# A q load moved behind a transpose, and eight mask transfers moved to ScalarE's queue, in a decayed attention followed by a feed-forward layer

## The chip, the cores and the metric

The kernel runs on one core of a Trainium2 chip. The metric is the device time of one execution in microseconds. Before the change it is 207.12 us, the median of three runs (206.98 to 209.63).

## What is computed

A causal linear attention with a decay for each head is followed by a feed-forward layer with a parametric ReLU. Cut to what matters:

```
q, k, v: (4, 8, 768, 64)            # batch, heads, sequence, head size, float32
for each block of 64 positions:
    intra = ((q k^T) * lam^(i - j), zero above the diagonal) v
    inter = (q * lam^(i + 1)) state
    out   = intra + inter
    state = lam^64 * state + (k * lam^(63 - i))^T v
x = out as (3072, 512)
h = x @ w_in                        # (512, 2048)
g = max(h, 0) + alpha * min(h, 0)
result = g @ w_out                  # (2048, 512)
```

## The kernel before

The work is cut into 6 chunks of 512 rows of x. Chunk c holds 256 positions of two batches. A chunk's attention has four units, one for each batch of the chunk and each half of the heads: units 16 to 19 are chunk 4 (the last chunk but one), 16 and 17 its first batch, 18 and 19 its second.

For each unit, q and k are loaded as float32 (`load`, lines 82 to 102), cast to float16 (`cast`), transposed by a DMA (`transposes(n, "D")`, line 378), and q times its decay is formed from the transposed tile (`decayed`, L422). `cluster(old, new)` then runs on TensorE (PE): `inter(old)` (L442), the scores of the new unit (L472, or L460 in chunks 4 and 5), `intra(old)` (L506), and the new unit's state products (L526). VectorE (DVE) multiplies the scores with a mask (L487, L485) and updates the states R (L555); ScalarE (ACT) copies the old unit's result into xT (L298). `inter` of a unit reads states that the cluster before it has updated, so it also waits for that cluster's copy into xT and its updates of R.

The feed-forward layer fills the time between clusters: `up(c, f)` is four matmuls (L635) into one PSUM bank, ACT's negated ReLU `m` (L643) and DVE's combination `g` (L650), which frees the bank. The banks are "tk", "op" and two of "h". `down(c, t, part, 4)` is four matmuls with w_out (L663); after the last part ACT copies the sums out (L676) and SyncE's queue (SP) stores them (L679). The order on each engine is the order of the calls, which are written out by hand one after another up to chunk 2's end, and by a table `plan` after that. Each engine works through its list in order, and a DMA's issue is an instruction in the list of the engine that issues it.

Chunks 4 and 5 take the rows of a unit in another order than the others, and need masks in that order. `half_mask(0)` makes the first of them with four transfers from `dmask` into a tile of its own, which later units with the first half of the heads use; `half_mask(1)` makes the second with four transfers from `dmask` into the half of `dmask` that is no longer read after `masked(14)`. `later_half` (L264), on GpSimd (POOL), then fills the last quarter of each from the transferred part. Before the change all eight are issued by SP.

Transfers that SP and ACT issue report their end through eight semaphores that are handed out in turn to both queues together. A transfer is not issued before the previous one with the same semaphore has landed, so the issuing engine may wait for that at the place of the issue.

Names used below: T14 to T17 are the transposes of units 14 to 17; Q is the q load of chunk 4's second batch (512 KB) and K the four k loads of that batch (128 KB each); S1 and S2 are the stores after `down(1, 2, 3)` and `down(1, 3, 3)`; M0a to M0d are the four transfers of `half_mask(0)` and M1a to M1d those of `half_mask(1)`.

Of the kernel before, what the change touches and what calls it, by code (L numbers as in the profile page):

```python
# [11 lines left out]
def kernel(  # L12
# [16 lines left out]
    nc = tc.nc  # L29
    ctx.enter_context(tc.manual_schedule())  # L30
    fp32 = mybir.dt.float32
# [5 lines left out]
    B, H, S, D = q.shape  # L37
    assert (B, H, S, D) == (4, 8, 768, 64)
    L = 128
# [10 lines left out]
    raw_pool = ctx.enter_context(tc.tile_pool(name="raw", bufs=5))  # L50
# [31 lines left out]
    def load(c, bi, x, half=None, queue="S"):  # L82

        pb, b = c // 2, 2 * (c % 2) + bi
        if (c, bi) not in raws:
            raws[c, bi] = {}
        if x not in raws[c, bi]:
            raws[c, bi][x] = raw_pool.tile([128, H, 2 * D], fp32, tag=f"{x}raw", name=f"{x}raw")
        heads = ds(0, H) if half is None else ds(4 * half, 4)
        i = "kqv".index(x)  # L90
        if x == "k" and c >= HC:
            for a in range(2):
                for f in range(2):
                    nc.sync.dma_start(  # L94
                        out=raws[c, bi][x][ds(64 * a, 64), heads, ds(D * f, D)],
                        in_=k[b, heads, ds(pb * W + L * a + 64 * f, 64), :].rearrange("h p d -> p h d"),
                    )
            return
        (nc.gpsimd if queue == "G" else nc.sync).dma_start(  # L99
            out=raws[c, bi][x][:, heads, :],  # L100
            in_=(k, q, v)[i][b, heads, ds(pb * W, W), :].rearrange("h (p e) d -> p h (e d)", e=2),
        )
# [39 lines left out]
    def bank_of(bank, name, dtype=fp32):  # L142
        pool = h_ps_pool if bank == "h" else ps
        return pool.tile([128, CH], dtype, tag=bank, name=name)
# [25 lines left out]
    for half in range(2):  # L170
# [7 lines left out]
        out=drop, in0=rel_i, scalar1=0.0, scalar2=-1e30, op0=ALU.is_lt, op1=ALU.mult  # L178
# [65 lines left out]

    HM = {}

    def half_mask(hh):

        m = [dmask[:, x].rearrange("p l h a j -> p (l h) (a j)") for x in range(2)]
        if hh == 0:  # L250
            t = raw_pool.tile([128, H, 2 * D], fp32, tag="vraw", name="hmask")
            HM[0] = t.rearrange("p h d -> p (h d)")[:, 0:768].rearrange("p (x j) -> p x j", j=192)
        else:
            HM[1] = m[0]
        for a in range(2):
            for e in range(2):
                nc.sync.dma_start(
                    out=HM[hh][64 * a + e : 64 * a + 64 : 2, :, 0:L],
                    in_=m[hh][ds(64 * a, 32), :, ds(64 * (1 - e), L)],
                )  # L260

    def later_half(hh):

# [32 lines left out]
    def copy_on(eng, out, in_):  # L296
        if eng == "A":
            nc.scalar.activation(out, in_, AF.Copy)  # L298
        elif eng == "V":
            nc.vector.tensor_copy(out=out, in_=in_)  # L300
        else:
            nc.gpsimd.tensor_copy(out=out, in_=in_)  # L302
# [47 lines left out]
    def engine(x):  # L350
        return nc.gpsimd if x == "G" else nc.vector
# [21 lines left out]
    def transposes(n, eng, decay=True):  # L373

        t = T[n]
        qkT = qkt_pool.tile([128, 2, 2, 2, L], fp16, tag="qkT", name="qkT")
        if eng == "D":
            nc.sync.dma_start(  # L378
                out=qkT.rearrange("p x e h j -> p (x e h) j"),
                in_=t["qk16"].rearrange("p x e h d -> p (x e h d)"),  # L380
                transpose=True,
            )
        else:
            tp = ps.tile([128, 2, 2, 2, L], fp16, tag="tk", name="tp")
            for x in (1, 0):
                for e in range(2):
                    for hp in range(2):
                        nc.tensor.transpose(
                            tp[:, x, e, hp, :],
                            t["qk16"][:, x, e, ds(2 * hp, 2)].rearrange("p l d -> p (l d)"),  # L390
                            ident,
                        )
            copy_on(eng, qkT, tp)
            t["qps"] = tp[:, 0]
        t["qkT"] = qkT
        if decay:
            decayed(n)
# [19 lines left out]
    def decayed(n, eng="G"):  # L417
        c, bi, hh = units[n]
        t = T[n]
        qdT = qkt_pool.tile([128, 2, 2, L], fp16, tag="qdT", name="qdT")  # L420
        p = ds(64, 64) if c < 2 else ds(0, L)
        engine(eng).tensor_tensor(  # L422
            out=qdT[:, :, :, p],
            in0=(t["qps"] if eng == "P" else t["qkT"][:, 0])[:, :, :, p],
            in1=qdecay[:, hh, :, :, p],
            op=ALU.mult,
        )
        t["qdT"] = qdT
# [6 lines left out]
    def inter(n):  # L435
        co, bo, ho = units[n]
        pbo, bb = co // 2, 2 * (co % 2) + bo
        for a in range(2):
            if 2 * pbo + a == 0:
                continue  # L440
            for hp in range(2):
                nc.tensor.matmul(  # L442
                    ot[a][:, hp, :].rearrange("p (e j) -> p e j", e=2),
                    lhsT=R[bb, ho, 2 * pbo + a][:, hp].rearrange("p l d -> p (l d)"),
                    rhs=T[n]["qdT"][:, :, hp, ds(a * 64, 64)],
                    start=(hp == 0),
                    stop=False,
                    skip_group_check=True,
                )
# [118 lines left out]
    def cluster(old, new, eng="A"):  # L568

        if old is not None:  # L570
            inter(old)
        if new is not None:
            score_products(new)
        if old is not None:
            intra(old)
        if new is not None:
            state_products(new, kv_acc, old is None)
            masked(new)
        if old is not None:
            attended(old, eng)  # L580
        if new is not None:
            states(new, kv_acc)
# [47 lines left out]
    def up(c, f, bi=None, bank="h"):  # L630
        h_ps = bank_of(bank, "h_ps")
        n = CH if bi is None else W
        for gi in range(NHP):
            x = XT[c][:, gi]
            nc.tensor.matmul(  # L635
                h_ps[:, 0:n] if bi is None else h_ps[:, 0:n].rearrange("p (e j) -> p e j", e=2),
                lhsT=w_in_sb[:, gi, ts(f, 128)],
                rhs=x.rearrange("p e b j -> p (e b j)") if bi is None else x[:, :, bi, :],
                start=(gi == 0),
                stop=(gi == NHP - 1),  # L640
            )
        m = m_pool.tile([128, CH], fp32, tag="m", name="m")
        nc.scalar.activation(m[:, 0:n], h_ps[:, 0:n], AF.Relu, scale=-1.0)  # L643
        g = g_of(c, f)
        if bi is None:
            g, mv, hv = g.rearrange("p e b j -> p (e b j)"), m, h_ps
        else:
            g = g[:, :, bi, :]
            mv, hv = (y[:, 0:n].rearrange("p (e j) -> p e j", e=2) for y in (m, h_ps))
        nc.vector.scalar_tensor_tensor(  # L650
            out=g, in0=mv, scalar=oma[:, f : f + 1], in1=hv, op0=ALU.mult, op1=ALU.add
        )
# [4 lines left out]
    def down(c, t, part, nparts, bank="op"):  # L657
        if part == 0:
            O[c, t] = bank_of(bank, "o_ps")
        o_ps = O[c, t]  # L660
        n = NF // nparts
        for f in range(part * n, part * n + n):
            nc.tensor.matmul(  # L663
                o_ps,
                lhsT=lhs(c, f, t),
                rhs=w_out_sb[:, f, :],
                start=(f == 0),
                stop=(f == NF - 1),
            )
        if part == nparts - 1:  # L670
            store(c, t, o_ps, 0, DM)
            del O[c, t]
# [376 lines left out]
    cast(12, "q16", "G")  # L1049
    decayed(10, "G")  # L1050
    down(1, 1, 1, 4, "h")
    down(1, 0, 1, 4, "tk")
    load(4, 0, "q", 0)
    cast(13, "k16", "G")
    down(1, 2, 0, 4, "h")
    down(1, 2, 1, 4, "h")
    down(1, 1, 2, 4, "h")
    decayed(11, "G")
    cluster(9, 10, "A")
    cast(16, "q16", "G")  # L1060
# [20 lines left out]
    transposes(14, "D", False)  # L1081
    down(1, 2, 3, 4, "h")
    load(4, 0, "q", 1)
    half_mask(0)
    cast(15, "k16", "G")
    cast(17, "q16", "G")
    load_vh(4, 0, 0)
# [8 lines left out]
    key_decayed(17, "G")  # L1096
    up(2, 2, None, "h")
    up(2, 0, None, "tk")
    load(4, 1, "q", None)
    cast(17, "k16", "G")  # L1100
    decayed(14, "G")
    cast(16, "k16", "G")
    load_vh(4, 1, 0)
    cluster(12, 13, "A")
    load(4, 1, "k", None)
    transposes(16, "D", False)
    down(1, 3, 2, 4, "op")
    up(2, 1, None, "h")
    load_vh(4, 1, 1)
# [5 lines left out]
    key_decayed(18, "G")  # L1115
    cluster(13, 14, "A")
    down(1, 3, 3, 4, "op")
    half_mask(1)
    up(2, 10, None, "h")
    up(2, 13, None, "h")  # L1120
    up(2, 11, None, "op")
    cluster(14, 15, "A")
    up(2, 12, None, "h")
    up(2, 3, None, "tk")
    up(2, 6, None, "h")
    up(2, 9, None, "op")
# [111 lines left out]
```

## Time and profile before

| | |
|---|---|
| median of three runs | 207.12 us |
| the profiled execution's own time | 206.72 us |
| its span, first to last instruction | 204.9 us |
| PE busy | 198.6 us, 97% of the span |
| DVE busy | 154.9 us, 76% |
| POOL busy | 116.1 us, 57% |
| ACT busy | 113.8 us, 56% |
| clock granted to PE | full speed in all slices |

The views of the profile give times from the start of the span. Between span and execution time lie 1.8 us that no instruction of the kernel fills. A row of the timeline is: start, duration, engine, line, operation, names of output and inputs, count, and in brackets the idle time before it with what ended it. SPq and ACTq rows are issues of transfers; the transfer itself goes on after its issue.

### The profile page before, as it was taken

What the parts mean: (1) busy time and instruction counts of PE and PEld (TensorE: products, weight loads), DVE (VectorE), ACT (ScalarE), POOL (GpSimd) and SP (SyncE); (2) the same over time, 40 slices, a digit from 0 to 9 for tenths busy, and PEclk for the clock granted to TensorE, in tenths of its full rate; (3) what the DMA queues carried; (4) which work ended last, traced back from release to release, by engine and by line L of the source; (5) the groups of instructions that cost most, each with busy time, mean ns of one, the idle gap of its engine ahead of it and who ended that gap; (6) DMA issues with size and microseconds to landing.
All of it is one profiled execution on the core that took longest, in us unless ns stands there. A gap on an engine that the chain in (4) does not pass through costs nothing.

```text
span 204.9 us, 5641 instructions
## 1 busy us (share of the span) xinstructions
PE 198.6 (97%) x2271; PEld 121.2 (59%) x2271; DVE 154.9 (76%) x289; ACT 113.8 (56%) x212; POOL 116.1 (57%) x145
## 2 busy tenths in 40 slices
PE   7999999999999999999799999999999999999993
PEld 6776445556445465555454554467666666666883
DVE  6988889578789647899977679958888467675831
ACT  7986778144777118656486466654453544534320
POOL 8999893054478991299286957982085040553000
PEclk9999999999999999999999999999999999999999
DMA  5999999997999996899999995381001111011123
GB/s 165 278 196 234 248 264 207 234 293 230 230 261 282 201 231 156 226 154 218 180 242 140 263 151 79 65 128 37 18 0 54 51 54 51 3 51 55 62 88 110
DMA packets 67871, 31.71 MB, mean 155 GB/s; under 512 B 39860, under 2 KB 65604, under 8 KB 67844
## 3 DMA queue, kind: packets, MB, share of 16 engines
q1 hardware_dynamic: 48180, 21.64, 47.2%
q0 software_dynamic: 19360, 9.57, 33.0%
q8 instruction: 18, 0.29, 0.6%
q10 hardware_dynamic: 304, 0.13, 0.2%
q14 instruction: 9, 0.07, 0.1%
HBM read 27.27 MB, written 6.29 MB: 164 GB/s over the span
## 4 chain that ended last, share of the span: by engine, by line
PE 86%; DMA 4%; DVE 3%; SPq 3%; ACT 1%; issue 1%; ACTq 0%
PE h_ps L635 36%; PE o_ps L663 20%; PE o_ps L745 18%; DMA qkT<-qk 4%; PE acc L506 2%; PE s L472 2%; PE acc L442 2%; PE tpx L408 2%; SPq L94 1%; DVE dmask L212 1%; PE s L460 1%; PE acc L526 1%; SPq L378 1%; SPq L99 1%; ACT L190 1%
## 5 line engine op out<-in xcount | busy, mean ns | idle before, releaser
L650 DVE SCALAR_TENSOR_TENSOR g<-m,oma,h_ps 128x512 f16<-128x512 f32 (+1 forms) x98 | 71.4, 736 | 28.7 <-ACT m L643 25.5
L635 PE MATMUL h_ps<-xT,w_in_sb 128*128 128x512 f16 (+1 forms) x392 | 92.0, 375 | 0.0
L643 ACT ACTIVATE m<-h_ps 128x512 f32<-128x512 f32 (+1 forms) x98 | 57.3, 588 | 46.8 <-PE h_ps L635 35.9
L635 PEld LDWEIGHTS <-w_in_sb 128*128 128x128 f16 x392 | 37.6, 98 | 37.0
L663 PE MATMUL o_ps<-w_out_sb,g 128*128 128x512 f16 x192 | 46.8, 380 | 0.0
L745 PEld LDWEIGHTS <-g 128*128 128x128 f16 x296 | 28.2, 98 | 8.2
L663 PEld LDWEIGHTS <-g 128*128 128x128 f16 x192 | 17.6, 98 | 19.4 <-DVE g L650 0.2
L728 POOL TENSOR_TENSOR s<-g 128x512 f16<-128x512 f16 x11 | 12.8, 1168 | 28.4 <-PE o_ps L745 16.1
L487 DVE TENSOR_TENSOR sm<-s,dmask 128x1024 f16<-128x1024 f32 x16 | 19.6, 1222 | 11.7 <-PE s L472 11.7
L298 ACT ACTIVATE xT<-acc 128x512 f16<-128x512 f32 x24 | 14.3, 597 | 24.1 <-PE acc L526 22.1
L422 POOL TENSOR_TENSOR qdT<-qkT,qdecay 128x512 f16<-128x512 f16 (+1 forms) x19 | 20.1, 1065 | 7.9 <-DMA qkT<-qk 4.7
L745 PE MATMUL o_ps<-w_out_sb,g 128*128 128x256 f16 x192 | 24.1, 273 | 0.0
L302 POOL CAST qk<-qraw 128x512 f16<-128x512 f32 x12 | 8.5, 707 | 18.3 <-DMA qraw<-in_q_dram 17.8
L555 DVE SCALAR_TENSOR_TENSOR R<-R,rdecay,acc 128x128 f16<-128x128 f16 x54 | 15.5, 342 | 0.1
L728 POOL TENSOR_TENSOR g<-g 128x512 f16<-128x512 f16 x11 | 13.2, 1199 | 0.9
L777 ACT ACTIVATE o_sb<-o_ps 128x512 f32<-128x512 f32 (+1 forms) x15 | 7.5, 497 | 7.6 <-PE o_ps L745 7.6
L358 POOL TENSOR_TENSOR kdec<-kraw,kdecay 128x512 f16<-128x512 f32 x10 | 10.7, 1082 | 1.1 <-DMA kraw<-in_k_dram 1.0
L335 POOL DMA_DIRECT2D v<-in_v_dram x16 | 11.1, 701 | 0.4 <-issue 0.4
L745 PE MATMUL o_ps<-w_sum,g 128*128 128x256 f16 x88 | 11.3, 273 | 0.0
L780 DVE TENSOR_TENSOR o_sb<-o_sb,o_ps 128x512 f32<-128x512 f32 (+1 forms) x12 | 6.5, 550 | 4.2 <-PE o_ps L745 2.2
L302 POOL CAST qk<-kraw 128x512 f16<-128x512 f32 x9 | 5.5, 614 | 6.9 <-DMA kraw<-in_k_dram 6.9
L506 PE MATMUL acc<-sm,v 64*64 64x128 f16 (+1 forms) x384 | 9.2, 214 | 0.0
(95 smaller groups left out, 219.7 us busy)
## 6 DMA issues: line engine op xcount, KB each, us to landing
out_dram<-o_sb SPq DMA_DIRECT2D x20, 256.0 KB, 2.9
qraw<-in_q_dram SPq DMA_DIRECT2D x6, 512.0 KB, 6.2
w_in_sb<-in_moe_w_in_dram POOLq DMA_DIRECT2D x4, 512.0 KB, 7.9
w_out_sb<-in_moe_w_out_dram POOLq DMA_DIRECT2D x4, 512.0 KB, 10.5
kraw<-in_k_dram SPq DMA_DIRECT2D x16, 128.0 KB, 4.9
kraw<-in_k_dram SPq DMA_DIRECT2D x3, 512.0 KB, 4.2
qraw<-in_q_dram POOLq DMA_DIRECT2D x6, 256.0 KB, 7.1
qraw<-in_q_dram SPq DMA_DIRECT2D x6, 256.0 KB
```

Of the source, the lines that this page charges most:

```text
L298: nc.scalar.activation(out, in_, AF.Copy)
L302: nc.gpsimd.tensor_copy(out=out, in_=in_)
L422: engine(eng).tensor_tensor(out=qdT[:, :, :, p], in0=(t["qps"] if eng == "P" else t["qkT"][:, 0])[:, :, :, p], in1=qdecay[:, hh, :, :, p], ...
L487: nc.vector.tensor_tensor(out=t["sm"].rearrange("p a h x j -> p (a h) x j"), in0=t["s"].rearrange("p a h x j -> p (a h) x j"), in1=mask_of ...
L506: nc.tensor.matmul(o, lhsT=t["v16"][p, 2 * hp + hl, e, :], rhs=x, start=(2 * pb + a == 0 and hp == 0 and e == 0), stop=(e == 1), skip_grou ...
L555: nc.vector.scalar_tensor_tensor(out=R[b, hh, m + 1][:, hp], in0=R[b, hh, m][:, hp], scalar=rdecay[:, 2 * hh + hp : 2 * hh + hp + 1], in1= ...
L635: nc.tensor.matmul(h_ps[:, 0:n] if bi is None else h_ps[:, 0:n].rearrange("p (e j) -> p e j", e=2), lhsT=w_in_sb[:, gi, ts(f, 128)], rhs=x ...
L643: nc.scalar.activation(m[:, 0:n], h_ps[:, 0:n], AF.Relu, scale=-1.0)
L650: nc.vector.scalar_tensor_tensor(out=g, in0=mv, scalar=oma[:, f : f + 1], in1=hv, op0=ALU.mult, op1=ALU.add)
L663: nc.tensor.matmul(o_ps, lhsT=lhs(c, f, t), rhs=w_out_sb[:, f, :], start=(f == 0), stop=(f == NF - 1),)
L728: engine(eng).tensor_tensor(out=out, in0=in0, in1=in1, op=op)
L745: nc.tensor.matmul(t[:, cols], lhsT=x, rhs=w, start=(fresh and f == 0), stop=(last and f == NF // 2 - 1), skip_group_check=True,)
```

## The change

Two things are moved. Q stands behind T16 in SP's list instead of ahead of K and T16. The eight mask transfers are issued by ACT instead of SP: M0a to M0d after `down(1, 1, 1)` and the `down` calls behind it (before: all four by SP, after the second half of the q load of chunk 4's first batch), and M1a to M1d one by one after the `up` calls (2, 10), (2, 13), (2, 11) and (2, 12) (before: all four by SP, after S2). What the transfers move is the same.

```
-    def half_mask(hh):
+    def half_mask(hh, a, e):
...
-        for a in range(2):
-            for e in range(2):
-                nc.sync.dma_start(
-                    out=HM[hh][64 * a + e : 64 * a + 64 : 2, :, 0:L],
-                    in_=m[hh][ds(64 * a, 32), :, ds(64 * (1 - e), L)],
-                )
+        nc.scalar.dma_start(
+            out=HM[hh][64 * a + e : 64 * a + 64 : 2, :, 0:L],
+            in_=m[hh][ds(64 * a, 32), :, ds(64 * (1 - e), L)],
+        )
...
     down(1, 1, 1, 4, "h")
+    half_mask(0, 0, 0)
...
     down(1, 2, 0, 4, "h")
+    half_mask(0, 0, 1)
     down(1, 2, 1, 4, "h")
+    half_mask(0, 1, 0)
     down(1, 1, 2, 4, "h")
+    half_mask(0, 1, 1)
...
     load(4, 0, "q", 1)
-    half_mask(0)
...
-    load(4, 1, "q", None)
+    load(4, 1, "k", None)
...
-    load(4, 1, "k", None)
     transposes(16, "D", False)
+    load(4, 1, "q", None)
...
     down(1, 3, 3, 4, "op")
-    half_mask(1)
     up(2, 10, None, "h")
+    half_mask(1, 0, 0)
     up(2, 13, None, "h")
+    half_mask(1, 0, 1)
     up(2, 11, None, "op")
+    half_mask(1, 1, 0)
     cluster(14, 15, "A")
     up(2, 12, None, "h")
+    half_mask(1, 1, 1)
```

In the changed program the order of the list on ACT from 93 us of the profile before on is: m of up(2, 10), M1a, m of (2, 13), M1b, m of (2, 11), M1c, xT of unit 14, m of (2, 12), M1d, m of (2, 3), (2, 6) and (2, 9), xT of unit 15. The semaphores handed out in turn make M0d wait for the landing of the v load of chunk 3's first batch, M1a and M1b for the first and third of K, M1c for T16, and M1d for S2. SP's list there is: S1, T15, K, T16, Q, S2, T17.

More of the change, by code (lines that the diff above doesn't have):

```diff
@@ L245 @@
     HM = {}
-    def half_mask(hh):
+    def half_mask(hh, a, e):
         m = [dmask[:, x].rearrange("p l h a j -> p (l h) (a j)") for x in range(2)]
[L250 to L254, printed above, removed]
-        for a in range(2):
-            for e in range(2):
-                nc.sync.dma_start(
-                    out=HM[hh][64 * a + e : 64 * a + 64 : 2, :, 0:L],
-                    in_=m[hh][ds(64 * a, 32), :, ds(64 * (1 - e), L)],
-                )
+        if hh not in HM:
+            if hh == 0:
+                t = raw_pool.tile([128, H, 2 * D], fp32, tag="vraw", name="hmask")
+                HM[0] = t.rearrange("p h d -> p (h d)")[:, 0:768].rearrange("p (x j) -> p x j", j=192)
+            else:
+                HM[1] = m[0]
+        nc.scalar.dma_start(
+            out=HM[hh][64 * a + e : 64 * a + 64 : 2, :, 0:L],
+            in_=m[hh][ds(64 * a, 32), :, ds(64 * (1 - e), L)],
+        )
     def later_half(hh):
```

## Prediction

> **What bounds the kernel now.** I read the page's busy line first, then PE's waits, the chain that ended last, and then the timelines of the engines around the one wait that PE has.
>
> ```profile
> span 204.9 us, 5641 instructions
> PE 198.6 (97%) x2271; PEld 121.2 (59%) x2271; DVE 154.9 (76%) x289; ACT 113.8 (56%) x212; POOL 116.1 (57%) x145
> PE s L460 <- DMA qkT<-qk: 1.3, 1, 1.3
> 92.78 8.05 DMA qkT<-qk
> ```
>
> PE is idle for 204.9 - 198.6 = 6.3 us in all. The longest single wait is the 1.3 us for one transpose (third line, from PE's waits), whose transfer is on the chain for 8.05 us, from 92.78 to 100.83. The matmuls themselves are untouched by this change, so I expect nothing to be won beyond these 1.3 us. The question is whether they are won, and what the moved issues cost on their new engine.
>
> ```profile
> 95.75 3.63 PE L635 MATMUL h_ps<-xT,w_in_sb 128*128 128x512 f16 x16
> 99.22 0.39 PE L442 MATMUL acc<-qdT,R 128*128 128x128 f16 x4
> 100.87 0.37 PE L460 MATMUL s<-qkT 64*64 64x128 f16 x16 [1.27 <-DMA qkT<-qk]
> 101.52 1.90 PE L635 MATMUL h_ps<-xT,w_in_sb 128*128 128x512 f16 x8
> 105.85 0.39 PE L442 MATMUL acc<-qdT,R 128*128 128x128 f16 x4
> ```
>
> On PE the waiting instruction is the scores of unit 16, so the transpose is T16. The row at 95.75 is the four `up` calls (2, 12), (2, 3), (2, 6), (2, 9); 99.22 is `inter(15)`; the row at 101.52 begins with `up(2, 7)`, which uses bank "tk" after `up(2, 3)`. I take the start of `up(2, 7)`, 101.52, as the mark: by how much it moves, the end moves, as PE has no idle gap of note after it.
>
> **What holds T16.** The issues on SP, then POOL.
>
> ```profile
> 82.24 0.44 SPq L99 DMA_DIRECT2D qraw<-in_q_dram  x1
> 82.73 2.63 SPq L257 DMA_DIRECT2D hmask<-dmask  x4
> 85.47 0.54 SPq L679 DMA_DIRECT2D out_dram<-o_sb  x1
> 86.15 1.44 SPq L378 DMA_TRANSPOSE qkT<-qk  x1
> 87.63 1.42 SPq L99 DMA_DIRECT2D qraw<-in_q_dram  x1
> 89.09 3.51 SPq L94 DMA_DIRECT2D kraw<-in_k_dram  x4
> 92.78 2.80 SPq L378 DMA_TRANSPOSE qkT<-qk  x1
> 95.68 0.53 SPq L679 DMA_DIRECT2D out_dram<-o_sb  x1
> 96.31 3.58 SPq L257 DMA_DIRECT2D dmask<-dmask  x4
> ```
>
> ```profile
> 77.10 0.61 POOL L302 CAST qk<-kraw 128x512 f16<-128x512 f32 x1
> 85.59 0.61 POOL L302 CAST qk<-qraw 128x512 f16<-128x512 f32 x1 [7.88 <-DMA qraw<-in_q_dram]
> 92.03 0.62 POOL L302 CAST qk<-kraw 128x512 f16<-128x512 f32 x1
> 92.58 2.75 POOL L335 DMA_DIRECT2D v<-in_v_dram  x4
> 103.31 0.40 POOL L264 COPY dmask<-dmask 128x256 f32<-128x256 f32 x1 [4.46 <-DMA dmask<-dmask]
> ```
>
> SP works almost without a gap from 82 to 100 us, so its list decides when each issue comes. But T16 has a second condition: its k half is cast by POOL at 92.03 to 92.65, and T16 is issued at 92.78. Both are ready within 0.1 us of each other. POOL's list up to that cast starts when the q load issued at 82.24 lands (85.59), and that load is not moved.
>
> **The change part by part.** *SP loses M0 and, ahead of T16, Q.* That is 2.63 + 1.42 = 4.05 us: K is issued by about 88.6 instead of 92.6, as T15 has its cast since 77.7. T16 gains nothing at its issue, since the cast still ends at 92.65: I keep 92.65. What T16 gains is an emptier queue. Before, K and Q were issued in the 5 us ahead of it, and its issue alone took 2.80; now K has 4 us more to drain and Q comes behind.
>
> ```profile
> 67.12 1.24 SPq L378 DMA_TRANSPOSE qkT<-qk  x1
> 71.62 1.16 POOL L422 TENSOR_TENSOR qdT<-qkT,qdecay 128x512 f16<-128x512 f16 x1 [0.42 <-DMA qkT<-qk]
> DMA to landing us min/median/max: 3.8/5.9/6.4
> ```
>
> The quickest transpose with a known landing took 3.8 us from issue, the slowest 6.4 (the third row, all transposes of the trace for which it is known), T16 itself 8.05; the one issued at 67.12 let POOL go on at 71.62, 4.5 us later. Four v loads by POOL still run beside T16 (issued from 92.58). I take 4.5, so T16 lands at 97.2, with 96.45 and 100.7 as ends. By this PE's wait would be gone, as PE reaches the scores at 99.6.
>
> The Trainium skill, page "DMA: Bandwidth & Descriptors", section "Issuing engines are not separate DMA queues", speaks against this: transfers of all issuing engines run on the same 16 DMA engines and interleave, and another issuer saves issue time alone. By that rule alone T16 would take its 8.05 again, and the sum would be that of the second rival below. No row so far bears this out or against it: no two executions with another issuer can be compared yet.
>
> *M0 on ACT.* ACT is idle for 4.69 us where they stand:
>
> ```profile
> 62.65 1.52 SPq L99 DMA_DIRECT2D vraw<-in_v_dram  x2
> vraw<-in_v_dram SPq DMA_DIRECT2D x1, 512.0 KB, 5.5
> 68.24 0.60 ACT L643 ACTIVATE m<-h_ps 128x512 f32<-128x512 f32 x1 [1.56 <-PE h_ps L635]
> 73.52 0.60 ACT L298 ACTIVATE xT<-acc 128x512 f16<-128x512 f32 x1 [4.69 <-PE acc L526]
> ```
>
> M0d waits for a v load issued at 62.65 that takes 5.5, landing near 68.2, before ACT gets there at 68.84. Four issues at SP's price (2.63 / 4 = 0.66) end at 71.5; xT at 73.52 is not touched. ACT's own price of an issue is bounded below by nothing, where it lies beside the running activation, and above by the 2.80 that T16's issue took; 0.66, the same transfer on SP, is nearest. At the upper end four would need 11.2 us and delay xT, but no row shows a mask near that. Cost: 0. Their 256 KB run earlier, beside T11 and T12 instead of beside T15; POOL's idle 7.88 us before 85.59 takes up a delay of a microsecond there.
>
> *M1 on ACT.* This is where a wait is added. ACT's and DVE's rows:
>
> ```profile
> 93.22 0.60 ACT L643 ACTIVATE m<-h_ps 128x512 f32<-128x512 f32 x1 [0.27 <-PE h_ps L635]
> 94.94 0.60 ACT L643 ACTIVATE m<-h_ps 128x512 f32<-128x512 f32 x1 [0.27 <-PE h_ps L635]
> 95.88 0.60 ACT L298 ACTIVATE xT<-acc 128x512 f16<-128x512 f32 x1 [0.34 <-PE acc L526]
> 97.37 1.11 DVE L555 SCALAR_TENSOR_TENSOR R<-R,rdecay,acc 128x128 f16<-128x128 f16 x4
> 103.22 0.75 DVE L650 SCALAR_TENSOR_TENSOR g<-m,oma,h_ps 128x512 f16<-128x512 f32 x1 [0.36 <-ACT m L643]
> ```
>
> M1a and M1b (behind 93.22 and the next m) wait for parts of K that were issued 4 us or more earlier: they cost 0.66 each, partly inside the 0.27 gaps, and ACT reaches M1c at about 96.3 instead of 95.5. M1c waits for T16. Until 97.2 ACT stands, with xT of unit 14, and behind it DVE's updates of R (they come after that copy), and so `inter(15)`, queued. From T16's landing on: issue 0.66, xT 0.60, R 1.11, `inter(15)` 0.39, the rest of the cluster 101.52 - 100.87 = 0.65, and three hand-overs of 0.05 (T16's landing at 100.83 let PE start at 100.87): 3.56 in all. So `up(2, 7)` could start at 97.2 + 3.56 = 100.8, 0.7 earlier than before. This alone would still be a gain.
>
> M1d waits for S2. S2 is now issued behind T16 (1.3) and Q (1.42): about 95.4, the same as before. Behind M1d on ACT stand m of `up(2, 3)`, whose g frees bank "tk" for `up(2, 7)`. From S2's landing: issue 0.66, m 0.60, g 0.75, hand-overs 0.15: 2.16.
>
> ```profile
> DMA to landing us min/median/max: 2.3/2.3/2.3
> DMA to landing us min/median/max: 6.0/6.0/6.0
> 92.00:102.00 10.00, 8.73 (x129) 4.72 (x128) 9.60 (x18) 5.75 (x11) 6.85 (x10) 1.00 1.62 201
> ```
>
> When does S2 land? The first row is the store issued at 79.77, with little beside it: 2.3. The second is S2 itself in the trace: 6.0. So 97.7 and 101.4 are the ends. Between them I go by the bytes: from 92.65 on T16 (256 KB), four v loads (64 KB each), Q (512 KB), S2 (256 KB) and M1a and M1b (128 KB), together 1.44 MB in bytes, have to pass, and the third row shows 201 GB/s in these 10 us: 7.2 us, hence 99.85. A lone store of 262 kB needs 1.3 at that rate and took 2.3, so 1.0 of a transfer is not rate; half of that, as the queue runs already, gives 100.3, also the nearer to S2's own row. Then `up(2, 7)` starts at 100.3 + 2.16 = 102.46, later than the 100.8 of the other chain: +0.94 us.
>
> *What is late next.* xT of unit 15 follows m of (2, 3), (2, 6), (2, 9) and ends near 103.3, when `up(2, 7)` ends. M1d lands 3.8 after its issue (the median of the second masks; worst 5.4):
>
> ```profile
> DMA to landing us min/median/max: 3.0/3.8/5.4
> 103.67 2.28 POOL L422 TENSOR_TENSOR qdT<-qkT,qdecay 128x512 f16<-128x512 f16 x2
> ```
>
> From 100.3 that is 104.1; POOL's copy (0.40) and the first qdT (1.14) end at 105.7, before `inter(16)` at 105.85 + 0.94. T17 is issued earlier, near 96, and K is already in: no loss there.
>
> **Sum.** -1.26 (PE's wait on T16, 101.52 - 100.26, the time at which PE is ready when nothing holds it: 99.22 + 0.39 + 0.65), +2.20 (the wait moved to `up(2, 7)` through ACT, 102.46 - 100.26): +0.94 us on a span of 204.9, so 205.8; with the 1.8 around it 207.6 for that execution. The runs' median stands 0.4 above the profiled execution, so I forecast 208.0.
>
> **Rivals.** *First, the gain arrives.* If S2 lands by 98.0, both chains end before PE is ready at 100.26, with T16 at its quick end of 96.45: 1.26 saved, 205.9. S2 at 98.7 saves 0.7, at 99.36 nothing. For it: K is out of the way 4 us earlier, and a store alone took 2.3. Against it: Q now stands between T16 and S2, and POOL's loads do not move. Centre 206.5.
>
> *Second, slower.* T16 stays as slow as it was, 8.05, because the DMA engines and not the order of issue set its time. It lands at 100.7, ACT stands there, and Q and S2 (0.79 MB at 201 GB/s, 3.9 us) follow: S2 at 104.6, `up(2, 7)` at 106.8, +5.2 us: 212.3. It decides from T16's landing at 98.0 on, where 98.0 + 3.56 passes 101.52 whatever S2 does; with S2 at its old 6.0 it is +2.0, 209.1. Against it: T16's time held K's and Q's remainder, which is gone.
>
> *Third, the masks come too late.* M1d issued at 100.3 takes the worst 5.4: POOL's qdT ends at 107.3, `inter(16)` 0.5 later still: +1.4, 208.5.
>
> **How the numbers follow.** Forecast 0.50 (207.2 to 209.1), gain 0.30 (205.9 to 207.1), second rival 0.12 (209.1 to 212.3), third 0.08. The range is 206.0 to 210.0: it holds the forecast, the third rival, nearly all of the gain and the near end of the second. A difference of 2%, 4.1 us, is about what a measurement of this kernel can tell from no change. A gain of that size is three times PE's whole wait: 0.01. A loss of that size needs the far half of the second rival: 0.05. Within 2%: 0.94.
>
> **What would show it.** Right: PE's wait for the transposed tile at the scores of unit 16 is gone or under 0.3; T16 is issued near 92.7, in about 1.3, and lands near 97; ACT is idle before M1c until T16's landing and before M1d until S2's; PE waits before `up(2, 7)` for g. T16 issued before 92 would show that POOL's cast did not hold it. Wrong: ACT not idle at M1c and M1d, a T16 of 8 us, or an end moved by more than `up(2, 7)` moved, which would mean a cost that I have not seen.

## The result and the profile after

The changed kernel takes 214.29 us (median of four runs, 213.6 to 214.65), the kernel before 207.05 us on the same chip. The ratio is 1.036, 95% interval 1.032 to 1.040: slower by 3.6%. The forecast was 208.0, with a range of 206.0 to 210.0; the direction was right and the size was not. The profiled execution took 214.65 us, with a span of 212.9: 8.0 more than before. Medians are of all executions, and ratios leave out those over 1.5% above the fastest of their kernel.

The page of the kernel after, its busy line and its slices, and PE's waits:

```profile
span 212.9 us, 5638 instructions
PE 202.0 (95%) x2271; PEld 123.1 (58%) x2271; DVE 156.8 (74%) x289; ACT 113.7 (53%) x212; POOL 115.7 (54%) x145
PEclk9999999999999999999669999999999999999999
PE h_ps L634 <- DVE g L649: 3.3, 1, 3.3
PE acc L441 <- DVE R L554: 1.2, 1, 1.2
```

PE's wait for the transposed tile (1.3 us) is gone from its list. In its place stand two waits, 1.2 and 3.3 us. And there is something that was in no slice of before: PE's clock falls to 0.6 in two slices. PE is busy 3.4 us longer with the same 2271 matmuls, as some of them ran slower: in the warm-up, and where the clock fell.

The timeline of PE in the kernel after, around the mark of the prediction, `up(2, 7)`:

```profile
96.44 3.63 PE L634 MATMUL h_ps<-xT,w_in_sb 128*128 128x512 f16 x16
101.26 0.38 PE L441 MATMUL acc<-qdT,R 128*128 128x128 f16 x4 [1.19 <-DVE R L554]
101.99 0.29 PE L525 MATMUL acc<-v,kdec 64*64 64x64 f16 x8
105.62 3.57 PE L634 MATMUL h_ps<-xT,w_in_sb 128*128 128x512 f16 x8 [3.34 <-DVE g L649]
108.99 1.49 PE L662 MATMUL o_ps<-w_out_sb,g 128*128 128x512 f16 x4
110.31 1.03 PE L634 MATMUL h_ps<-xT,w_in_sb 128*128 128x512 f16 x4
```

Against the rows of before this gives the ledger. The `up` calls at 95.75 begin at 96.44: 0.7 of the difference had arisen by 10 us in the warm-up and belongs to the execution (other executions below have between 0.0 and 0.6 there). `inter(15)` waits 1.19 for R. `up(2, 7)` begins at 105.62 instead of 101.52: +4.1. Its eight matmuls take 3.57 instead of 1.90 us, and the row of 104.12 comes at 110.31: +6.2. So 2.1 us are the clock; all four executions of this kernel have a mean granted clock of 0.982 to 0.984. Up to PE's last matmul another 0.3 is added. The last 1.5 lie behind it, in the final stores (4.8 us from PE's end at 208.1 to the span's end, 3.3 before), and no other execution profiled here has them. Without the start's 0.7 and these 1.5 the ledger comes to 5.8 us, while the four executions lie 6.5 to 7.6 above the 207.05 of the kernel before; what the other three lose beyond the 5.8 is not shown.

The clock fell early in the longer stretch:

```profile
103.00:104.00 1.00, 0.00 (x0) 0.00 (x0) 0.00 (x0) 0.00 (x0) 0.00 (x0) 0.54 1.32 182
```

The third figure from the end is the clock. It was full up to 103 and averages 0.54 from 103 to 104, so it had halved about 0.8 us after PE stopped at 102.28. The stretch of 1.19 us just before it may count too.

ACT's timeline of the kernel after shows where the waits come from, and the chain that ended last names their first link:

```profile
94.84 0.61 ACTq L256 DMA_DIRECT2D dmask<-dmask  x1
98.64 0.61 ACTq L256 DMA_DIRECT2D dmask<-dmask  x1
99.36 0.60 ACT L297 ACTIVATE xT<-acc 128x512 f16<-128x512 f32 x1 [3.07 <-PE h_ps L634]
103.48 0.61 ACTq L256 DMA_DIRECT2D dmask<-dmask  x1
104.19 1.57 ACT L642 ACTIVATE m<-h_ps 128x512 f32<-128x512 f32 x3 [3.75 <-DMA out_dram<-o_sb]
```

```profile
95.66 7.79 DMA out_dram<-o_sb
103.48 0.61 ACTq L256
104.19 0.60 ACT m L642
104.82 0.76 DVE g L649
105.62 3.57 PE h_ps L634 x8
```

M1c is issued at 98.64 and M1d at 103.48. Ahead of M1c ACT stands 3.07 us; PE, which the row names, had been done long before, so the releaser is another: T16, whose semaphore the issue waits for and which landed at 98.62 by the events in the trace. Ahead of M1d it stands 3.75 us, and there the row names the store. S2 was issued at 95.66 and was under way for 7.79 us.

### The profile page after: what moved, and what is told of

It is laid out like the page before. It is cut to its first block, busy times and chain, and to the rows that moved or that the text cites. A ratio compares the mean times of both kernels' runs of the same rounds, so it can differ in the third digit from the quotient of the medians.

```text
span 212.9 us, 5638 instructions
## 1 busy us (share of the span) xinstructions
PE 202.0 (95%) x2271; PEld 123.1 (58%) x2271; DVE 156.8 (74%) x289; ACT 113.7 (53%) x212; POOL 115.7 (54%) x145
## 4 chain that ended last, share of the span: by engine, by line
PE 89%; DMA 4%; DVE 2%; ACT 2%; ACTq 1%; issue 0%
PE h_ps L634 38%; PE o_ps L662 19%; PE o_ps L744 17%; DMA out_dram<-o_sb 4%; PE unread L162 3%; PE acc L505 2%; PE s L471 2%; PE acc L441 2%; PE tpx L407 2%; DVE w_sum L710 1%; DVE g L649 1%; PE acc L525 1%; PE s L459 1%; ACT L190 1%; ACT m L642 1%; PE p L744 0%
## 5 line engine op out<-in xcount | busy, mean ns | idle before, releaser
L634 PE MATMUL h_ps<-xT,w_in_sb 128*128 128x512 f16 (+1 forms) x392 | 93.6, 380 | 3.5 <-DVE g L649 3.3
L421 POOL TENSOR_TENSOR qdT<-qkT,qdecay 128x512 f16<-128x512 f16 (+1 forms) x19 | 21.2, 1119 | 6.6 <-DMA qkT<-qk 3.2
L301 POOL CAST qk<-qraw 128x512 f16<-128x512 f32 x12 | 7.6, 630 | 16.2 <-DMA qraw<-in_q_dram 15.4
L441 PE MATMUL acc<-qdT,R 128*128 128x128 f16 x80 | 8.4, 219 | 1.4 <-DVE R L554 1.2
```

The costliest lines, as they stand in the source:

```text
L421: engine(eng).tensor_tensor(out=qdT[:, :, :, p], in0=(t["qps"] if eng == "P" else t["qkT"][:, 0])[:, :, :, p], in1=qdecay[:, hh, :, :, p], ...
L441: nc.tensor.matmul(ot[a][:, hp, :].rearrange("p (e j) -> p e j", e=2), lhsT=R[bb, ho, 2 * pbo + a][:, hp].rearrange("p l d -> p (l d)"), r ...
L634: nc.tensor.matmul(h_ps[:, 0:n] if bi is None else h_ps[:, 0:n].rearrange("p (e j) -> p e j", e=2), lhsT=w_in_sb[:, gi, ts(f, 128)], rhs=x ...
```

## The experiments

**What belongs to which part.** Four kernels on one chip, beside a kernel before of 206.79 us. The first moves Q alone:

```
 load(4, 1, "k", None)          # kernel before; was: load(4, 1, "q", None)
 ...
 transposes(16, "D", False)
+load(4, 1, "q", None)
```

> The kernel before, with Q alone moved behind T16; all masks stay on SP's queue. Theory (the loss is ACT standing at M1c and M1d): ACT issues nothing here, so nobody waits for S2. T16 is still held by POOL's cast until about 92.7 but has K and no Q ahead of it, so PE's wait of 1.27 us for it shrinks: 205.8 to 207.0 us. Rival (Q in front of S2 is bad by itself, whoever waits): 209 us or more.

Measured: 207.14 us, ratio 1.005 (1.001 to 1.008). PE and the chain of this kernel:

```profile
99.61 0.37 PE L460 MATMUL s<-qkT 64*64 64x128 f16 x16
105.69 0.38 PE L442 MATMUL acc<-qdT,R 128*128 128x128 f16 x4 [0.93 <-POOL qdT L422]
```

```profile
98.49 5.26 DMA dmask<-dmask
104.30 1.35 POOL qdT L422
```

```profile
DMA to landing us min/median/max: 7.8/7.8/7.8
```

The wait for T16 is gone; the scores begin at 99.61 instead of 100.87. But the masks behind Q and S2 land at 103.75 (98.49 + 5.26), POOL's qdT is late, and `inter(16)` gives 0.93 back. The last row is S2 here: 7.8 us, as in the kernel after, but no computing engine waits for it. So Q's place makes S2 late, and by itself it gives back through the masks about what it wins. By the median the rival (209 and more) falls, and the theory was 0.1 us too low. Three of the ten executions took 208.67 to 209.54, which this trace, of the fastest, does not explain.

The second kernel is the changed one with Q back in its old place:

```
-load(4, 1, "k", None)
+load(4, 1, "q", None)
 ...
+load(4, 1, "k", None)
 transposes(16, "D", False)
-load(4, 1, "q", None)
```

> The kernel after, with Q back ahead of K and T16; the masks are issued by ACT as in the changed kernel. By the turn of the semaphores M1c now waits for the last part of K, long landed, and M1d still for S2, which has no Q ahead of it any more. Theory (the loss is S2's late landing seen through M1d, and T16's seen through M1c): S2 is issued near 94 to 95 and lands within 3 to 6 us, so up(2,7) starts between 100 and 103 instead of 105.6, PE's idle stays under 2.5 us and the clock full: 206.5 to 208.5 us. Rival (eight transfers on ACT's queue cost it by themselves): 212 us or more.

Measured: 210.17 us, ratio 1.017 (1.013 to 1.021): between the two. ACT, PE and DVE of this kernel:

```profile
100.54 0.61 ACTq L256 DMA_DIRECT2D dmask<-dmask  x1
```

```profile
102.68 1.89 PE L634 MATMUL h_ps<-xT,w_in_sb 128*128 128x512 f16 x8 [2.04 <-DVE g L649]
107.68 0.38 PE L441 MATMUL acc<-qdT,R 128*128 128x128 f16 x4 [0.52 <-POOL qdT L421]
```

```profile
112.69 4.54 DVE L710 TENSOR_TENSOR w_sum<-w_out_sb 128x512 f16<-128x512 f16 x1
```

M1d goes out at 100.54, three microseconds earlier than in the kernel after, and `up(2, 7)` starts at 102.68 with a gap of 2.04 and at full clock, all as the theory had it. The number missed by 1.7, through two delays further on. The masks cost 0.5. And a w_sum on DVE takes 4.54 us; g stands behind it, and PE waits 1.3 us for that. In the kernel before DVE has for the same operation:

```profile
110.86 0.42 DVE L711 TENSOR_TENSOR w_sum<-w_out_sb 128x512 f16<-128x512 f16 x1
```

By the medians Q alone costs 0.35 us and the masks alone 3.4; together they cost 7.2. So about 3.5 us come only when both are moved: Q directly ahead of S2, and M1d behind S2.

The third kernel leaves M0 on ACT and Q behind T16, and gives M1 back to SP:

```
 down(1, 3, 3, 4, "op")
+half_mask(1, ...) x4 on nc.sync
 ...                            # the four calls on nc.scalar taken out
```

> The kernel after, with the second masks M1a to M1d back on SP behind S2; M0 stays on ACT and Q behind T16. Theory: neither ACT nor PE waits for T16 or S2 at M1; PE's old wait of 1.27 us for T16 is gone too: 205.6 to 206.4 us, PEclk full between 100 and 110 us. Rival (Q's place or M0 on ACT carries part of the loss): 208 us or more.

Measured: 209.59 us median of 12 runs (206.61 to 210.09), ratio 1.006 (1.003 to 1.010); the profiled execution took 209.91. The median lies in the rival's range. PE's row and a window behind it:

```profile
107.36 0.38 PE L441 MATMUL acc<-qdT,R 128*128 128x128 f16 x4 [2.29 <-POOL qdT L421]
```

```profile
108.00:110.00 2.00, 2.00 (x36) 0.86 (x22) 1.47 (x3) 0.60 (x1) 2.00 (x3) 0.56 1.38 219
```

Both waits of ACT are gone, as the theory had it, and `up(2, 7)` starts at 100.58. Then the masks, again last behind Q and S2, hold qdT of unit 16, PE waits 2.29 us, and the clock falls to 0.56. So Q's place carries part of the loss, as the rival had it, through the masks. Late masks are what the prediction's third rival was about, with a chance of 0.08, though by a slow M1d on ACT.

The trace stands for the slower executions alone: seven of the twelve took 209.55 to 210.09 at a mean clock of 0.989 to 0.992, and five took 206.61 to 208.20 at 0.998 to 1.0. In this trace T16 was issued at 93.86, against 92.73 with Q alone moved, and all that follows on SP came later too; whether M0 on ACT has a share in that was not tried.

The fourth keeps M1 on ACT, but so early that by the turn of the semaphores it follows transfers that have landed. (There M1 overwrites a mask that unit 14's scores still use, so part of the computation is changed.)

```
 later_half(0)
+half_mask(1, 0, 0); half_mask(1, 0, 1); half_mask(1, 1, 0); half_mask(1, 1, 1)
```

> The kernel after, with M1a to M1d written behind the first half's copy, ahead of up(2,10); they stay on ACT. Their places in the turn of the semaphores now follow S1, T15 and the first two parts of K, all landed by then. Theory (the wait, not the queue, is the cost): four issues of 0.6 us beside the activations, no ACT idle over 1 us in 90 to 104, PE's wait for T16 gone: 205.6 to 206.8 us. Rival (masks on ACT's queue in this stage cost PE by themselves): 209 us or more.

Measured: 209.4 us, ratio 1.011 (1.007 to 1.015). The number is the rival's; the trace shows that the kernel is no test of it. ACT, then PE, then DVE of this kernel:

```profile
91.12 2.63 ACTq L256 DMA_DIRECT2D dmask<-dmask  x4
93.86 0.60 ACT L297 ACTIVATE xT<-acc 128x512 f16<-128x512 f32 x1 [2.20 <-DMA dmask<-dmask]
```

```profile
95.00 1.02 PE L634 MATMUL h_ps<-xT,w_in_sb 128*128 128x512 f16 x4 [0.36 <-ACT o_sb L675]
98.33 0.40 PE L441 MATMUL acc<-qdT,R 128*128 128x128 f16 x4 [2.31 <-DVE R L554]
99.35 5.31 PE L634 MATMUL h_ps<-xT,w_in_sb 128*128 128x512 f16 x16
```

```profile
96.02 1.23 DVE L486 TENSOR_TENSOR sm<-s,dmask 128x1024 f16<-128x1024 f32 x1 [3.58 <-PE h_ps L634]
97.16 1.11 DVE L554 SCALAR_TENSOR_TENSOR R<-R,rdecay,acc 128x128 f16<-128x128 f16 x4
```

No issue waits. The four of them in a row keep ACT for 2.63 us, xT starts at 93.86, and PE waits 0.36 us at 95.00 for what ACT does next. PE's 2.31 us have another cause. DVE's masking of unit 14 now stands behind the four transfers that write its mask, and waits for all of them: by the events in the trace the last landed at 95.94, and the masking starts at 96.02. The matmul that its row names is not what it needs. R follows at 97.16 and `inter(14)` at 98.33, and the 16 matmuls behind it run at a lower clock: 5.31 us instead of 3.63. So the 2.31 us are not the price of issues on ACT, and this kernel leaves open what issues without a wait cost PE beyond the 0.36 us.

**Which wait.** One slot earlier in the order, M1d follows T16 instead of S2; the four transfers and ACT's queue are the same.

```
 down(1, 3, 3, 4, "op")
+half_mask(1, 0, 0); half_mask(1, 0, 1)
 up(2, 10, None, "h")
+half_mask(1, 1, 0)
 up(2, 13, None, "h")
+half_mask(1, 1, 1)
```

> The kernel after, with the second masks on ACT a little earlier in the order: M1a and M1b right behind down(1,3,3), M1c behind up(2,10), M1d behind up(2,13). By the turn of the semaphores M1a now follows S1, M1b and M1c parts of K, all landed, and M1d follows T16 instead of S2. Theory (it is the semaphore's turn that chains ACT to S2): ACT stands once, until T16 lands near 98, not until S2 near 103; inter(15) starts near 102, PE's idle is one gap of about 2 us and no second one before up(2,7): 207.5 to 210.5 us, the upper part if that gap is enough to halve the clock. Rival (ACT is held by the transfers' share of the queues, whatever their turn): two gaps as in the kernel after, 213 us or more.

Measured: 209.87 us, ratio 1.015 (1.012 to 1.018). ACT and PE of this kernel:

```profile
98.60 0.61 ACTq L256 DMA_DIRECT2D dmask<-dmask  x1
```

```profile
104.22 1.89 PE L634 MATMUL h_ps<-xT,w_in_sb 128*128 128x512 f16 x8 [0.20 <-DVE g L649]
```

ACT stands once, until 98.60, and goes through; nothing waits for S2. `up(2, 7)` starts 1.4 earlier than in the kernel after and at full clock, and the kernel is 4.4 us faster by the medians. The theory holds in this, and the rival falls. It had expected one gap of about 2 us on PE; there are two, of 1.8 and 1.2 us.

Next, S2 ahead of Q, with M1d still behind S2:

```
 transposes(16, "D", False)
-load(4, 1, "q", None)
 ...
 up(2, 10, None, "h")
+load(4, 1, "q", None)
```

> The kernel after, with Q moved one place further on SP: behind S2 instead of directly behind T16. By the turn of the semaphores M1c now follows the last part of K and M1d still follows S2. Theory (S2 lands late because Q's 512 KB stand directly ahead of it): S2 is issued near 94.7 and lands in 5.5 to 6.0 us, at 100.2 to 100.7, instead of 7.79 us and 103.45; up(2,7) starts 2.2 later, near 102.6, one gap of 2 us: 207.0 to 209.0 us. Rival (S2 is late because the v loads and T16 fill the queues, with Q or without): S2 takes over 7 us, up(2,7) starts at 104 or later: 210.5 us or more.

Measured: 209.68 us median of 10 runs (207.36 to 211.5), ratio 1.010 (1.006 to 1.014); the profiled execution is the fastest, 207.36. In it, SP, ACT and PE:

```profile
94.23 0.79 SPq L678 DMA_DIRECT2D out_dram<-o_sb  x1
```

```profile
99.66 0.61 ACTq L256 DMA_DIRECT2D dmask<-dmask  x1
```

```profile
101.80 1.89 PE L634 MATMUL h_ps<-xT,w_in_sb 128*128 128x512 f16 x8 [1.40 <-DVE g L649]
```

S2 takes 5.4 us (99.66 - 94.23) instead of 7.8, and `up(2, 7)` starts 3.8 earlier than in the kernel after. So about 2.4 us of S2's time is Q directly ahead of it. The other 5.4 remain without Q; the theory had 5.5 to 6.0 for that. The landings in all the traces agree: S2 took 7.2 to 9.0 us in the eight profiled kernels with Q directly ahead of it, and 5.4 to 6.0 in the five others, the kernel before among them.

The median lies 0.7 above the theory's range. Six of the ten executions took 209.64 to 211.5 at a mean clock of 0.989 to 0.992, and four took 207.36 to 208.95 at 0.997 to 1.0. The profile is of the fastest, so what lowered the clock in the six is not shown.

**The clock.** The changed kernel, with matmuls that nobody reads put where PE stands idle; ACT's waits are untouched.

```
 decayed(16, "G")
+fill(5, "s")                   # second kernel; fill(10, "s") in the third
 cluster(15, 16, "A")
+fill(12, "h")                  # all three
 up(2, 7, None, "tk")
```

> The kernel after, with 12 more matmuls of 128x512 (their result is read by nobody) put on PE ahead of up(2,7), where PE stood idle for 3.34 us. ACT, DVE and the transfers are as in the kernel after, so the chain S2, M1d, m, g, up(2,7) is not shortened. Theory (2 us of the loss are PE's clock, which halves behind the idle stretch): PE is busy in the gap for 12 x 0.215 = 2.6 us, PEclk stays full from 100 to 110, up(2,7) takes 1.9 instead of 3.57 us: 211.9 to 212.8 us. Rival (the clock dip has another cause, or costs nothing on the path): 213.8 to 215 us.

> The kernel after, with 12 matmuls of 128x512 ahead of up(2,7) as in the first filling and 5 more ahead of inter(15), where PE stands too (1.19 us in the kernel after, 2.51 in the execution with one filling); their results are read by nobody, and ACT's waits stay as they are. Theory (PE's idle stretch halves its clock): neither gap is left long enough, PEclk is full from 98 to 112, and up(2,7) starts when its g is there, near 105.5: the loss of 2.05 us by the clock is gone and nothing else, span 210.3 to 211.3, 211.5 to 212.6 us in the median, below that of the first filling or the same. Rival (the filling shortens something else, or the clock dips without an idle stretch): a clock under 0.9 in a window from 98 to 112, or up(2,7) starting more than 1 us away from 105.6.

> As the kernel with both fillings, but with 10 matmuls instead of 5 ahead of inter(15): there PE still stood 1.97 us behind the first filling, as T16 landed at 100.19, and the clock halved all the same. Ten take 2.15 us. Theory (an idle stretch of about 2 us and more halves PE's clock): PE idles less than 1 us at either place, PEclk is 1.00 in every window from 98 to 112, up(2,7) takes 1.9 us and starts when g is there; what is left of the loss is ACT's two waits: a span of 209.5 to 211.5, a median of 211.0 to 212.5 us. Rival (the clock dips without an idle stretch): a window from 98 to 112 with a clock under 0.9.

Measured: 212.0, 211.93 and 211.64 us (ratios 1.024, 1.022, 1.021). The medians came as expected, but the first two traces do not show the cause cleanly: in the profiled executions T16 landed later (99.65 and 100.19), so PE stood longer ahead of `inter(15)`, and the clock halved behind that gap and under the filling. That is the case the second expectation gave to its rival: the clock was 0.50 in a window, and `up(2, 7)` started at 108.05. The third is clean. Its PE, and the second's beside it:

```profile
102.38 0.38 PE L441 MATMUL acc<-qdT,R 128*128 128x128 f16 x4 [0.66 <-DVE R L554]
103.34 2.76 PE L150 MATMUL unread<-ident 128*128 128x512 f16 x12
105.94 1.89 PE L634 MATMUL h_ps<-xT,w_in_sb 128*128 128x512 f16 x8
```

```profile
102.82 0.38 PE L441 MATMUL acc<-qdT,R 128*128 128x128 f16 x4 [1.97 <-DVE R L554]
103.78 4.43 PE L150 MATMUL unread<-ident 128*128 128x512 f16 x12
```

With no gap over 0.7 us the clock is full from 98 to 112; twelve matmuls take 2.76 us, where behind a gap of 1.97 they took 4.43. ACT still stands ahead of M1c and M1d (4.70 and 2.26 us), `up(2, 7)` starts 0.3 later than in the kernel after, and the kernel is still 2.6 us faster by the medians. All four of its executions have a mean clock of 1.0, where the four of the kernel after have 0.982 to 0.984. So PE's idle time itself makes the clock fall, and the 2.6 us fit the 2.1 read from the kernel after.

**A version that beats both.** If the masks are the next thing late, Q has to go behind them, and all on SP:

```
 half_mask(1)                   # kernel before
+load(4, 1, "q", None)          # and no longer ahead of K
```

> The kernel before, with Q alone moved, but further than in the change: behind T16, S2 and the second masks, all on SP. Theory (with Q directly behind T16 its 512 KB delay S2 and the masks behind it; put behind the masks it delays nothing that is waited for soon): T16 lands by 98.5, PE's 1.27 us wait for it is gone, the masks land by 102.5 instead of 103.7, the 0.93 us wait for qdT of unit 16 is gone too: 205.3 to 206.0 us against some 206.8 for the kernel before. Rival (T16's early landing is given back whatever follows): 206.5 to 207.5 us.

> The kernel with Q behind the second masks on SP, and in addition ACT's casts of unit 18 in the order k, q instead of q, k. There ACT stood 2.02 us for Q's landing at 104.48 with an m behind the cast, and PE then 0.71 us for its g. Theory: with k's cast first ACT stands about 0.6 us less, and most of PE's 0.71 us is gone: 205.3 to 206.1 us, against 206.3 without it. Rival (m is held all the same, or the order of the two casts does not matter): 206.1 to 206.7 us.

Measured: 206.32 us, ratio 0.997 (0.994 to 0.999), and with ACT's two casts exchanged 205.78 us, ratio 0.995 (0.992 to 0.998). Both are faster than the kernel before, by 0.3 and 0.5%, and the intervals leave out 1 by little. The first fell 0.3 short of the theory's range, and its trace says why: an m on ACT stands behind a cast that waits for Q, and PE waits 0.71 us for its g. The second is as expected. PE of the first, then of the second:

```profile
106.97 1.02 PE L635 MATMUL h_ps<-xT,w_in_sb 128*128 128x512 f16 x4 [0.71 <-DVE g L650]
```

```profile
100.20 1.90 PE L635 MATMUL h_ps<-xT,w_in_sb 128*128 128x512 f16 x8
104.52 0.39 PE L442 MATMUL acc<-qdT,R 128*128 128x128 f16 x4
```

In the second, `up(2, 7)` starts at 100.20, the 1.3 us that the prediction named as all there was to win, and they are kept: the row of 105.85 of the kernel before comes at 104.52.

## Why the prediction was right and wrong

*T16, near right.* It was issued at 93.38 (92.7 and the 0.7 of the start), right after POOL's cast, in 1.28 us. It landed by 98.6, 97.9 without the start, against 97.2. The wait on it went, as forecast. It took 5.24 us, and 4.4 to 6.6 in the other eleven changed kernels, where it landed between 97.7 and 100.2; the prediction's 4.5 was at the quick end, and the 8.05 of the kernel before never came back.

*M0 on ACT at no cost, right as far as one trace shows.* In the kernel with Q behind S2, which also has M0 on ACT, the `up` calls at 95.75 begin at 95.91.

*M1c and the 3.56 us behind T16, right.* 98.62 + 3.56 = 102.18; PE was through the cluster at 102.28.

*S2's landing, the step that failed.* The prediction put it at 100.3, between 97.7 and 101.4; it was 103.45, 102.75 without the start, past its own upper end. From there on the sum was exact: 103.45 + 2.16 = 105.61, and `up(2, 7)` started at 105.62. S2 was issued about when the prediction had it (94.96 without the start, against 95.4), so the term that was mis-sized is S2's time under way: 4.9 us in the sum, 7.79 measured. The upper end of 6.0 was S2's own row in the kernel before, but there Q had landed at 93.8, before S2 was issued. With Q directly ahead no trace has it under 7.2.

The sum over the bytes let 1.44 MB flow from 92.65 on at 201 GB/s. Two windows of the kernel after, the second up to S2's landing (the last figure is GB/s):

```profile
92.00:95.00 3.00, 3.00 (x19) 1.35 (x16) 3.00 (x7) 1.97 (x4) 3.00 (x5) 1.00 0.22 14
95.00:103.45 8.45, 6.09 (x115) 3.48 (x114) 4.75 (x9) 2.10 (x4) 4.56 (x6) 0.98 1.36 197
```

The rate was right; the start and the bytes were not. From 92 to 95 only 14 GB/s were moved: K had drained, T16, Q and S2 all stood behind POOL's cast, and what was issued from 93.3 on began to pass near 95. From there to S2's landing 197 GB/s are 1.66 MB, 1.70 with the 0.04 before. That is 0.26 more than the sum counted; T17 and M1c were issued meanwhile. By an estimate from these figures, 1.2 of the 2.45 us that S2 came too late are the start (94.3 without the execution's 0.7, against 92.65 and the half microsecond that the prediction allowed), and 1.3 are the bytes.

That the queues were empty is not what makes S2 late. The first window with Q alone moved, with Q behind S2, and with Q behind the second masks:

```profile
92.00:95.00 3.00, 3.00 (x18) 1.45 (x16) 2.96 (x7) 1.88 (x4) 3.00 (x6) 1.00 1.03 163
92.00:95.00 3.00, 3.00 (x17) 1.37 (x15) 2.90 (x7) 1.95 (x4) 3.00 (x6) 1.00 0.37 31
92.00:95.00 3.00, 3.00 (x15) 1.35 (x15) 3.00 (x7) 2.09 (x4) 3.00 (x5) 1.00 1.37 210
```

With Q alone moved K was still passing, at 163 GB/s, and S2 took the same 7.79 us. With Q behind S2 the queues moved 31 and S2 took 5.41; with Q behind the masks they moved 210 and S2 took 5.53. So Q's place decides, and whether the queues were idle before does not. The Trainium skill, page "DMA: Bandwidth & Descriptors", section "Queues, rings and completion order", says that a completion signal lands only after every earlier write of the same DMA engine, across its queues. The runs agree with it: S2 took 5.4 us with T16 and POOL's loads ahead of it, 7.8 with Q there as well.

*The clock, missing from the sum.* The prediction found the end moved by as much as `up(2, 7)`; it moved by 2.1 us more, as eight matmuls took 3.57 us and the next four 1.49. The prediction put the clock at nothing without a reason: it asked only how long PE would wait, not what the wait does to PE. The Trainium skill, page "TensorE: Matmul & The Clock Gate", section "Why this matters for your kernels", advises against gaps over some 3 us. The gap here was 3.34, but shorter ones did the same (2.51, 2.31, 2.29, 1.97), while 2.04 and 1.77 in two other executions did not; the measurement decides, and 2 us are to be feared.

*The second rival, near in time and wrong in cause.* Its 212.3 was nearest. It needed a T16 of 8.05 us, which was 5.24; S2 was late without it. With T16 in time the prediction let S2 land at 101.4 at the latest, so the case that came was in none of its sums. The nearness is luck: the rival has no loss by the clock.

*The third rival* does not show in the kernel after, where PE came later than the masks. It decides where ACT's waits are taken away. Its price was misread: the row with 3.8 as its median counts one of the first masks (3.0) beside two of the second (3.8 and 5.4). M1d took 5.03 us in the kernel after, by the events in the trace.

## What to carry to other kernels

A transfer put on a computing engine's queue brings along the wait for whatever transfer held its semaphore before; look up which one that is, where it lands in the new order, and what stands behind it on that engine. Price a landing from a transfer that had the same neighbour directly ahead of it: S2's own 6.0 us held only while Q stood elsewhere. A sum over bytes starts when bytes begin to pass, here some 1.7 us after the first issue (93.3 to 95), and counts what is issued meanwhile too. And a gap of about 2 us or more on PE costs its own length and, in four kernels here, 1.7 to 2.1 us more in clock. Before a kernel counts as a test, look whether its edit makes anything else wait: a transfer written earlier in the program is also waited for by whatever reads its target after it.

## What was not expected of the hardware

- PE's clock halved at idle stretches of 1.97 to 3.34 us, and twelve matmuls ran in 4.43 instead of 2.76 us behind the shortest. In the kernel after it had halved some 0.8 us into the longest, which another of 1.19 us preceded. A stretch of 2.04 us left it alone, and executions of one kernel differ. What else decides was not tried.
- A 512 KB load directly ahead of a 256 KB store on SP's queue makes the store's landing some 2 us later (7.2 to 9.0 us against 5.4 to 6.0), whether the queues were idle before or not.
- One w_sum of 128x512 on DVE took 4.54 us in one kernel and 0.42 in the kernel before. POOL worked without a pause beside the long one; that this is the cause was not tried.
